# Three of six key chunks transposed by TensorE, one shared ring of four PSUM banks, and routing on GpSimd spread over later steps

## The chip, the cores and the metric

The kernel runs on one core of a Trainium2 chip. What counts is the device time of one launch, in microseconds (us). The core has a matrix engine (TensorE, PE in the profile), three engines for elementwise work (VectorE: DVE, ScalarE: ACT, GpSimd: POOL), a queue processor (SyncE: SP) and 16 DMA engines. Each engine runs its own list of instructions in the order in which the program wrote them, and waits at an instruction until the semaphores that it names have been reached.

## The reference

The kernel fuses an attention with a routed two-layer network. Four batches of 12288 queries (C = 128) look at 768 keys each, which are 4 by 4 means of `kv` times `w_sr`:

```python
kv_pool = kv.reshape(B, H // r, r, W // r, r, C).mean(axis=(2, 4))
k = v = kv_pool.reshape(B, -1, C) @ w_sr
s = (q @ k.transpose(0, 2, 1)) / np.sqrt(C)
a = np.exp(s - s.max(-1, keepdims=True))
a /= a.sum(-1, keepdims=True) + 1e-09
x = (a @ v).reshape(B * N, C)
do_compute = x @ w_skip > 0
out = x.copy()
# rows with do_compute: the best of 8 experts by x @ w_gate
out[rows of e] += gate_w * (np.maximum(x[rows of e] @ w1[e], 0) @ w2[e])
```

## The kernel before, in words

**Stages.** From about 36 us to 1107 us a loop runs over 384 tiles of 128 queries (96 per batch). Each tile's attention is computed, its rows are written to `out`, and after every 12 tiles a group is routed: for each active row the expert and the place in that expert's list are worked out, and the rows are scattered into a scratch array in HBM. From 1107 to 1205 us a first piece of the experts runs, and a device loop does the rest up to 1964 us. The change touches the first stage, and beyond it only the banks from which the first piece of the experts takes its PSUM tiles.

**One step.** Step t of the loop works on several tiles at once; the order in the program is the order on each engine:

- PE: `scores(t)`, six f32 matmuls of 128 x 384 (L578 to L580) into `s_ps`, which holds two tiles; `attend(t-6)`, 18 f16 matmuls (L641) whose weights are the transposed probabilities; `p_transpose(t-1)` (L616).
- DVE: `nm`, the row maximum of `scores(t)` (L586); then `ptq` lo (L624), the inverse of the row sums `rs` (L649, L651) and `p` lo (L599).
- ACT: `q_hi` (L566, every fourth step), `ptq` hi (L623), `p` hi (L595), the scaling of finished rows (L656, two tiles at a time), the exponential `p_sb` (L591).
- SP: a DMA transpose of `p16` into `pt` (L603) each step, and the transfers of q, kv, out and of padding rows.
- POOL: `q_lo` (L567), sums over kv blocks (L437, not in all steps), the routing (L692 to L708, L721, L756 to L760), row numbers (L771, L772), and 12 scatters for each group (L183, two emitted per step).

**Two ways to turn a tile.** The probabilities of a tile are a 128 x 768 f32 array and must be turned, so that keys lie on partitions: six chunks of 128. Each is kept as a sum of two f16 values, hi and lo. `KD` chunks are split first (`p` hi by ACT, `p` lo by DVE, side by side in `p16`) and turned by a DMA; the other `KP = KC - KD` are turned in f32 by PE into a PSUM bank and split from there (`ptq` hi by ACT, `ptq` lo by DVE). `PP` tiles share one bank and one pair of split instructions.

**PSUM.** `s_ps` has four banks. Before, `ps_a` has three banks that serve in turn, one for the attention results of each pair of tiles and one for the PE transposes of each pair; `ps_m` has one bank, "misc", for routing (31 groups) and for the preparation of the next batch's keys. A tile's next owner waits until its last readers are done: for attention results these are L649 and the two L656, for transposes L623 and L624.

**Routing.** `route(r, ...)` is a generator; each `yield` ends its work for the step. Its product `oh_all` (L721, POOL) is the operand of two matmuls at the end of a later step (L748, L749 on PE), whose results go through `pre` (L752, DVE) and POOL to `di`, the row numbers for the scatters.

Of the kernel before, what the change touches and what calls it, by code (L numbers as in the profile page):

```python
# [9 lines left out]
F32 = mybir.dt.float32  # L10
# [5 lines left out]
ALU = mybir.AluOpType  # L16
# [8 lines left out]
def kernel(  # L25
# [40 lines left out]
    LAG = 6  # L66
    W1, W2, W3 = 3, 6, 0
    PSL = 11
    KD = 4
    PP = 2  # L70
    L1, L2, PW, PX = 11, 8, 1, 1
    ROW = C + 4

# [291 lines left out]
    with ExitStack() as p1:  # L365
# [3 lines left out]
        qt = p1.enter_context(tc.tile_pool(name="qt", bufs=3))  # L369
        pp = p1.enter_context(tc.tile_pool(name="pp", bufs=3))  # L370
        ptp = p1.enter_context(tc.tile_pool(name="ptp", bufs=LAG))
        ptq = p1.enter_context(tc.tile_pool(name="ptq", bufs=4))
        hl = p1.enter_context(tc.tile_pool(name="hl", bufs=4))
        small = p1.enter_context(tc.tile_pool(name="small", bufs=6))
        rowp = p1.enter_context(tc.tile_pool(name="rowp", bufs=3))
        rt = p1.enter_context(tc.tile_pool(name="rt", bufs=3))
        ps_a = p1.enter_context(tc.tile_pool(name="ps_a", bufs=3, space=PSUM))
        ps_m = p1.enter_context(tc.tile_pool(name="ps_m", bufs=1, space=PSUM))
        started = []

        def acc_ps():
            return ps_a.tile([P, 512], F32, name="acc_ps")

        def misc_ps():
            return ps_m.tile([P, 512], F32, name="misc") if started else acc_ps()
        p_kv = p1.enter_context(ExitStack())
        kvp = p_kv.enter_context(tc.tile_pool(name="kvp", bufs=4))
        p_s = p1.enter_context(ExitStack())
# [162 lines left out]
            q_sb[g] = qp.tile([P, GW], F32, name="q_sb")  # L551
            nc.sync.dma_start(q_sb[g], q[r][:, o * GT:(o + 1) * GT, :].rearrange("c t p -> c (t p)"))

        early_a, early_g, late_a, early_v, jobs = [], [], [], [], []
        LASTR = NTILE // RT - 1
        SNAPR = LASTR - 4

        def run_late(q):
            while q:
                q.pop(0)()  # L560

        def q_split(g):
            q_g = q_sb.pop(g)
            hi = qt.tile([P, GW], F32R, name="q_hi")
            lo = qt.tile([P, GW], F32R, name="q_lo")
            early_a.append(lambda: nc.scalar.copy(hi, q_g))  # L566
            early_g.append(lambda: nc.gpsimd.tensor_tensor(out=lo, in0=q_g, in1=hi.bitcast(F32), op=ALU.subtract))  # L567
            qT[g] = (hi, lo)

        def scores(t):  # L570
# [98 lines left out]
        def route(r, a, b, last, eng):  # L669
# [27 lines left out]
            if few:  # L697
                eng.scalar_tensor_tensor(out=ev, in0=d, scalar=0.0, in1=em(em8), op0=ALU.is_equal, op1=ALU.mult)
                eng.tensor_scalar(out=act, in0=rows[:, :, C], scalar1=0.0, scalar2=None, op0=ALU.is_gt)
                eng.scalar_tensor_tensor(out=na, in0=rows[:, :, C], scalar=0.0, in1=idt[:, 0:n], op0=ALU.is_le,  # L700
                                         op1=ALU.mult)
                ohb = oh_few[a // GT % 2]
            else:
                eng.tensor_scalar(out=ev, in0=d, scalar1=0.0, scalar2=None, op0=ALU.is_equal)
                eng.tensor_tensor(out=ev, in0=ev, in1=em(em8), op=ALU.mult)
                eng.tensor_scalar(out=act, in0=rows[:, :, C], scalar1=0.0, scalar2=None, op0=ALU.is_gt)
                eng.tensor_scalar(out=na, in0=act, scalar1=-1.0, scalar2=1.0, op0=ALU.mult, op1=ALU.add)
                eng.tensor_tensor(out=na, in0=na, in1=idt[:, 0:n], op=ALU.mult)  # L708
                oha = oh_all[r % 3]
                ohb = oha.rearrange("p e t -> p t e")[:, 1:RTP, :]  # L710
            yield
# [7 lines left out]
            oh = big_t("oh")  # L719
            nc.vector.tensor_tensor(out=oh, in0=em(em8), in1=bc(mn), op=ALU.is_equal)  # L720
            eng.tensor_tensor(out=ohb[:, 0:n, :], in0=oh, in1=bc(act), op=ALU.mult)  # L721
            for _ in range(1 if few else 2 if r < LASTR - 1 else K2):
                yield
            yield (None if r >= LASTR - 1 else GT - 1)
            while accs.get("done", 0) != r * RT + a:
# [9 lines left out]
            if few:  # L735
                ohf = ohb.rearrange("p t e -> p (t e)")
                nc.tensor.matmul(ps[:, 0:w + E], upper_bf, ohf[:, 0:w + E], start=True, stop=False)
                for j in range(n):
                    nc.tensor.matmul(ps[:, (j + 1) * E:w + E], ones_bf,
                                     ohb[:, j:j + 1, :].broadcast_to([P, n - j, E]), start=False, stop=(j == n - 1))  # L740
                nc.vector.tensor_tensor(out=nxt, in0=run, in1=ps[:, w:w + E], op=ALU.add)
                nc.vector.tensor_tensor(out=acc, in0=ps[:, 0:w].rearrange("p (t e) -> p t e", e=E), in1=em(run),
                                        op=ALU.add)
                nc.vector.tensor_scalar(out=gs, in0=gs, scalar1=1e-9, scalar2=x_sc, op0=ALU.add, op1=ALU.mult)
            else:
                wa = E * RTP
                ohf = oha.rearrange("p e t -> p (e t)")
                nc.tensor.matmul(ps[:, 0:wa], ones_bf, ohf, start=True, stop=True)  # L748
                nc.tensor.matmul(ps[:, wa:2 * wa], upper_bf, ohf, start=True, stop=True)  # L749
                yield  # L750
                pre = rt.tile([P, E, RTP], F32, name="pre")
                nc.vector.tensor_tensor_scan(pre.rearrange("p e t -> p (e t)"), keep.rearrange("p e t -> p (e t)"),  # L752
                                             ps[:, 0:wa], 0.0, ALU.mult, ALU.add)
                inner = ps[:, wa:2 * wa].rearrange("p (e t) -> p t e", t=RTP)[:, 1:RTP, :]
                nc.vector.tensor_tensor(out=acc, in0=inner, in1=pre.rearrange("p e t -> p t e")[:, 0:RT, :], op=ALU.add)
                eng.tensor_tensor(out=nxt, in0=run, in1=pre[:, :, RT], op=ALU.add)  # L756
                eng.tensor_scalar(out=gs, in0=gs, scalar1=1e-9, scalar2=x_sc, op0=ALU.add, op1=ALU.mult)
                eng.tensor_tensor(out=acc, in0=acc, in1=em(run), op=ALU.add)
            accs["done"] = r * RT + b
            eng.tensor_tensor(out=acc, in0=acc, in1=ohb[:, 0:n, :], op=ALU.mult)  # L760
            yield
            nc.vector.reciprocal(rows[:, :, C], gs)
            yield
            if r == SNAPR:
# [117 lines left out]
        q_split(0)  # L882
        q_split(1)
        run_late(early_a)
        warm(W1)
        kv_transpose(0, KC - 1, KC)
        run_late(early_g)
# [2 lines left out]
        warm(W3)  # L890
        preps = [prep_v(0)]
        next(preps[0])
        started.append(True)
        pools = []
        if SNAPR < 0:
            snapshot(None)
# [12 lines left out]
        while t < NTILE + LAG - 1 or jobs:  # L909
            t += 1  # L910
            b, tb = divmod(t, TPB)
            live = t < NTILE
            for now, nxt in ((split_a, next_a), (split_v, next_v), (late_a, next_l)):
                now.extend(nxt)
                nxt.clear()
            if live:
                scores(t)
            if 0 <= t - LAG < NTILE:
                attend(t - LAG)
            if 0 <= t - 1 < NTILE:  # L920
                p_transpose(t - 1)
            if live:
                row_max(t)
            run_late(early_a)
            run_late(split_a)
            if 0 <= t - 1 < NTILE:
                p_hi(t - 1)
            run_late(late_a)
            if live:
                row_exp(t)  # L930
            run_late(early_g)
            run_late(split_v)
            run_late(early_v)
            if 0 <= t - 1 < NTILE:
                p_lo(t - 1)
            if live:
                if t % GT == 0 and t // GT + RG < NGRP:
                    load_q(t // GT + RG)
                if b + 1 < B:
                    for k, r in KV_T.get(tb, ()):  # L940
                        load_kv(b + 1, k, [r])
                if b + 1 < B and tb == PREP_T:
                    preps.append(prep_kv(b + 1))
                if t in PAD_T:
                    write_pads(*PADS.pop(0))
            first_step(NTILE - t)
            if t == NTILE:
                p_s.close()
                p_kv.close()
                alloc_h(p1.enter_context(tc.tile_pool(name="hp1", bufs=1)))  # L950
                ps_up = p1.enter_context(tc.tile_pool(name="ps_up", bufs=4, space=PSUM))
                alloc["h"] = lambda: ps_up.tile([P, ST], F32, name="up_ps")
            ph = t % GT
            if ph == 1 and t // GT + 2 < NGRP:
                q_split(t // GT + 2)
            ranked = run_jobs(ph)
            if preps and not ranked and (ph in (0, 3) or tb < LAG):
                if next(preps[0], "end") == "end":
                    preps.pop(0)
            if live and b + 1 < B:  # L960
                for k, r in KV_T.get(tb - 4, ()):
                    if r == R - 1:
                        pools.append(pool_kv(b + 1, k))
                for _ in range(2 if tb >= 74 else 1):
                    if pools and next(pools[0], "end") == "end":
                        pools.pop(0)
            for _ in range(2 * (t >= NTILE)):
                next(first)
# [77 lines left out]
```

## Time and profile before

| | us |
|---|---|
| median of three runs (1979.64, 1980.99, 1993.7) | 1980.99 |
| profiled execution, whole | 1965.99 |
| its span | 1964.2 |
| loop over the tiles, 36 to 1107 us: PE / DVE / ACT / POOL busy | 974 / 899 / 810 / 752 of 1071 |
| first piece of the experts, 1107 to 1205 us: PE busy | 67 of 98 |
| loop over the experts, 1205 to 1964 us: PE busy | 744 of 759 |

Busy time is the time in which an engine worked on instructions; what lies between them is idle, and the trace names for each idle stretch the event that ended it ("issue" where it sees none, "remote" where the event was not the end of a recorded instruction). The granted clock ("PEclk") is the share of full speed at which PE was let run. In a row of a timeline the first number is the start, the second the length; "x2" means two instructions drawn as one, and the bracket at the end holds the idle time before them.

### The profile page before, as it was taken

Reading aid. Unit: us, or ns where it says so; the run is one execution under the profiler, and the core shown is the slowest. Engines: PE = TensorE matmul, PEld = TensorE weight load, DVE = VectorE, ACT = ScalarE, POOL = GpSimd, SP = SyncE. Lnnn points to the kernel's source line nnn. Section 1 sums busy time; section 2 is a strip of 40 time slices with the busy share of each in tenths; the row PEclk is TensorE's granted clock in tenths of the full one; section 3 lists DMA queues with packets and bytes.
Section 4 is the critical chain, followed back from the end, with each engine's and each line's share of the span. In section 5 each row is a group of like instructions: output and inputs, shape, how many; then the busy total and the mean of one; then the engine's idle time right before and its main releaser. Section 6 shows DMA issues by size and latency. Waiting matters only on the chain. (4 is left out here: it accounts for less than half of the span.)

```text
span 1964.2 us, 42746 instructions
## 1 busy us (share of the span) xinstructions
PE 1795.4 (91%) x13955; PEld 1284.2 (65%) x13955; DVE 1567.7 (80%) x3226; ACT 1325.5 (67%) x2484; POOL 1092.2 (56%) x1372
## 2 busy tenths in 40 slices
PE   4999978999898999898988768999999999999997
PEld 3988878988788888787887623444444444444443
DVE  7999967989877999686787736887878788878786
ACT  3878866878777878676776624666666666666664
POOL 2378864888857888656556552333333333333333
PEclk9999989999999999899999878999999999999999
DMA  7999978999888999799998613333333433333343
GB/s 173 205 199 213 202 164 165 211 180 187 158 160 167 201 205 208 159 195 183 180 181 187 133 50 104 92 97 92 97 90 99 111 98 93 95 94 95 90 99 90
DMA packets 621971, 284.88 MB, mean 145 GB/s; under 512 B 503168, under 2 KB 571904, under 8 KB 621824
## 3 DMA queue, kind: packets, MB, share of 16 engines
q1 hardware_dynamic: 600320, 244.56, 61.0%
q0 software_dynamic: 21504, 38.43, 6.8%
q8 instruction: 83, 1.36, 0.3%
q14 instruction: 64, 0.52, 0.1%
HBM read 90.60 MB, written 78.64 MB: 86 GB/s over the span
## 5 line engine op out<-in xcount | busy, mean ns | idle before, releaser
L183 POOL DMA_INDIRECT out_dram<-o,xin x288 | 295.9, 1028 | 494.9 <-DVE o L292 428.7
L591 ACT ACTIVATE p_sb<-s_ps,nm 128x768 f32<-128x768 f32 x384 | 346.9, 903 | 184.4 <-DVE nm L586 155.8
L183 POOL DMA_INDIRECT scr<-rows,di x384 | 394.9, 1028 | 135.4 <-issue 107.0
L586 DVE TENSOR_REDUCE nm<-s_ps 128x1 f32<-128x768 f32 x384 | 363.7, 947 | 125.0 <-PE s_ps L580 68.0
L269 DVE SCALAR_TENSOR_TENSOR h_lo<-h_ps,h_hi 128x512 f16<-128x512 f32 x544 | 344.1, 685 | 146.2 <-ACT h_hi L268 109.2
L641 PE MATMUL acc_ps<-v_hi,pt 128*128 128x138 f16 x3072 | 331.9, 228 | 48.1 <-DVE rs L649 24.1
L641 PEld LDWEIGHTS <-pt 128*128 128x128 f16 x4608 | 286.9, 100 | 121.1 <-issue 120.6
L268 ACT ACTIVATE h_hi<-h_ps 128x512 f16<-128x512 f32 x544 | 318.4, 597 | 51.2 <-PE h_ps L267 32.2
L599 DVE SCALAR_TENSOR_TENSOR p<-p_sb,p 128x512 f16<-128x512 f32 x384 | 318.2, 829 | 1.9 <-ACT p L595 1.4
L641 PE MATMUL acc_ps<-v_lo,pt 128*128 128x138 f16 x1536 | 302.6, 227 | 0.5 <-issue 0.5
L578 PE MATMUL s_ps<-k_hi,q_hi 128*128 128x384 f32 x768 | 299.2, 390 | 3.5 <-issue 3.4
L579 PE MATMUL s_ps<-k_lo,q_hi 128*128 128x384 f32 x768 | 265.4, 346 | 4.2 <-issue 4.0
L580 PE MATMUL s_ps<-k_hi,q_lo 128*128 128x384 f32 x768 | 264.3, 344 | 2.2 <-issue 2.2
L595 ACT ACTIVATE p<-p_sb 128x512 f16<-128x512 f32 x384 | 242.4, 631 | 7.4 <-DMA pt<-p 4.2
L265 PE MATMUL h_ps<-xT,w_hi 128*128 128x512 f16 x544 | 207.1, 381 | 6.0 <-issue 6.0
L266 PE MATMUL h_ps<-xT,w_hi 128*128 128x512 f16 x544 | 207.0, 380 | 0.0
L267 PE MATMUL h_ps<-xT,w_lo 128*128 128x512 f16 x544 | 206.9, 380 | 0.0
L281 PE MATMUL y_ps<-h_hi,w_hi 128*128 128x512 f16 x544 | 206.2, 379 | 0.0
L281 PE MATMUL y_ps<-h_hi,w_lo 128*128 128x512 f16 x544 | 206.2, 379 | 0.0
L281 PEld LDWEIGHTS <-w_hi 128*128 128x128 f16 x1152 | 113.4, 98 | 134.5 <-issue 4.0
L281 PE MATMUL y_ps<-h_lo,w_hi 128*128 128x512 f16 x544 | 195.1, 379 | 0.0
L284 ACT ACTIVATE yT<-y_ps,y_sc 128x512 f32<-128x512 f32 x68 | 46.7, 687 | 219.5 <-PE y_ps L281 219.5
(215 smaller groups left out, 3215.5 us busy)
## 6 DMA issues: line engine op xcount, KB each, us to landing
kvt<-in_kv_dram SPq DMA_DIRECT2D x96, 256.0 KB
q_sb<-in_q_dram SPq DMA_DIRECT2D x96, 256.0 KB
out_dram<-rows SPq DMA_DIRECT2D x96, 256.0 KB
xin<-scr SPq DMA_DIRECT2D x75, 264.0 KB, 2.9
w_raw<-in_moe_w_dram SPq DMA_DIRECT2D x38, 512.0 KB
scr<-pad SPq DMA_DIRECT2D x32, 264.0 KB
pt<-p SPq DMA_TRANSPOSE x384
scr<-rows,di POOLq DMA_INDIRECT x384
```

The costliest lines, as they stand in the source:

```text
L183: ins = nc.gpsimd.indirect_dma_start(out=dst, out_offset=bass.IndirectOffsetOnAxis(ap=ids, axis=0), in_=src, in_offset=None, bounds_check= ...
L268: nc.scalar.activation(out=h["hi"][:, c, :], in_=ps, func=AF.Relu)
L269: nc.vector.scalar_tensor_tensor(out=h["lo"][:, c, :], in0=ps, scalar=0.0, in1=h["hi"][:, c, :], op0=ALU.max, op1=ALU.subtract)
L281: nc.tensor.matmul(ps, w[:, c, :], h[x][:, c, :], start=(i == 0), stop=(i == len(terms) - 1))
L578: nc.tensor.matmul(s[:, h, :HK], q_hi, k_hi[:, sl], start=True, stop=False)
L579: nc.tensor.matmul(s[:, h, :HK], q_hi, k_lo[:, sl], start=False, stop=False)
L580: nc.tensor.matmul(s[:, h, :HK], q_lo, k_hi[:, sl], start=False, stop=True)
L586: nc.vector.tensor_reduce(out=NM[t], in_=S_PS[t][:, :, :HK], axis=AX.XY, op=ALU.max, negate=True)
L591: nc.scalar.activation(out=P_SB[t], in_=S_PS.pop(t)[:, :, :HK], func=AF.Exp, bias=NM.pop(t))
L595: nc.scalar.activation(out=P16[t][:, 0, :], in_=p_flat(t)[:, 0:KD * P], func=AF.Copy, scale=2.0 ** PEXP)
L599: nc.vector.scalar_tensor_tensor(out=p16[:, 1, :], in0=p_flat(t)[:, 0:KD * P], scalar=2.0 ** PEXP, in1=p16[:, 0, :], op0=ALU.mult, op1=ALU ...
L641: nc.tensor.matmul(ps[:, j % 2, :], w, v[a][:, k, :], start=(i == 0), stop=(i == len(AVL) - 1))
```

## The change

- `KD` goes from 4 to 3 and `PP` from 2 to 1: PE turns three chunks of every tile, not two; `ptq` is split for every tile (384 columns), not for every second (512); `p` hi, `p` lo and the DMA transposes work on 384 columns, not 512. `ptq` has 6 buffers in place of 4.
- `ps_a` and `ps_m` become one pool of four banks. Attention results, PE transposes and misc tiles take the next bank in turn.
- On ACT the scaling of finished rows comes ahead of `ptq` hi and `p` hi.
- `q_lo` is put into a list `next_g` that moves into `early_g` at the start of the following step.
- In `route`, `na` is one instruction; the part behind L752 (`nxt`, `gs`, `acc`) starts a step later, the reciprocal and the scatters two steps later; one more `yield` stands between `oh_all` and the matmuls.

```diff
-    KD = 4
-    PP = 2
+    KD = 3
+    PP = 1
...
-        ptq = p1.enter_context(tc.tile_pool(name="ptq", bufs=4))
+        ptq = p1.enter_context(tc.tile_pool(name="ptq", bufs=LAG))
...
-        ps_a = p1.enter_context(tc.tile_pool(name="ps_a", bufs=3, space=PSUM))
-        ps_m = p1.enter_context(tc.tile_pool(name="ps_m", bufs=1, space=PSUM))
-        started = []
-
+        ps_a = p1.enter_context(tc.tile_pool(name="ps_a", bufs=4, space=PSUM))
         def acc_ps():
             return ps_a.tile([P, 512], F32, name="acc_ps")
 
         def misc_ps():
-            return ps_m.tile([P, 512], F32, name="misc") if started else acc_ps()
+            return acc_ps()
...
             early_a.append(lambda: nc.scalar.copy(hi, q_g))
-            early_g.append(lambda: nc.gpsimd.tensor_tensor(out=lo, in0=q_g, in1=hi.bitcast(F32), op=ALU.subtract))
+            next_g.append(lambda: nc.gpsimd.tensor_tensor(out=lo, in0=q_g, in1=hi.bitcast(F32), op=ALU.subtract))
...
                 eng.tensor_scalar(out=act, in0=rows[:, :, C], scalar1=0.0, scalar2=None, op0=ALU.is_gt)
-                eng.tensor_scalar(out=na, in0=act, scalar1=-1.0, scalar2=1.0, op0=ALU.mult, op1=ALU.add)
-                eng.tensor_tensor(out=na, in0=na, in1=idt[:, 0:n], op=ALU.mult)
+                eng.tensor_scalar(out=na, in0=rows[:, :, C], scalar1=0.0, scalar2=float(BIG), op0=ALU.is_le, op1=ALU.mult)
...
-            for _ in range(1 if few else 2 if r < LASTR - 1 else K2):
+            for _ in range(1 if few else 3 if r < LASTR - 1 else K2):
                 yield
...
+                if r < LASTR - 1:
+                    yield
                 eng.tensor_tensor(out=nxt, in0=run, in1=pre[:, :, RT], op=ALU.add)
...
             yield
+            if not few and r < LASTR - 1:
+                yield
             nc.vector.reciprocal(rows[:, :, C], gs)
...
-            for now, nxt in ((split_a, next_a), (split_v, next_v), (late_a, next_l)):
+            for now, nxt in ((split_a, next_a), (split_v, next_v), (late_a, next_l), (early_g, next_g)):
...
             run_late(early_a)
+            run_late(late_a)
             run_late(split_a)
             if 0 <= t - 1 < NTILE:
                 p_hi(t - 1)
-            run_late(late_a)
             if live:
                 row_exp(t)
             run_late(early_g)
```

Lines behind the pools move up by three in the changed kernel (L721 becomes L717, L748 becomes L744).

On POOL, this stands before, for one group in the second batch, from the scatters of the group ahead of it (L183, `di`) over the routing's first part (L692 to L708) to `oh_all`:

```order
L183 DMA scr<-rows,di 409600x132 x2
L692 TENSOR_TENSOR d<-lg,mx 128x96
L704 TENSOR_SCALAR ev<-d 128x96
L705 TENSOR_TENSOR ev<-ev,em_80 128x96
L706 TENSOR_SCALAR act<-rows 128x12
L707 TENSOR_SCALAR na<-act 128x12
L708 TENSOR_TENSOR na<-na,idt 128x12
L183 DMA scr<-rows,di 409600x132 x6
L567 TENSOR_TENSOR q_lo<-q_sb,q_hi 128x512
L183 DMA scr<-rows,di 409600x132 x2
L721 TENSOR_TENSOR oh_all_94<-oh,act 128x12x8
L183 DMA scr<-rows,di 409600x132 x2
```

And this stands there in the changed kernel:

```order
L689 TENSOR_TENSOR d<-lg,mx 128x96
L701 TENSOR_SCALAR ev<-d 128x96
L702 TENSOR_TENSOR ev<-ev,em_80 128x96
L703 TENSOR_SCALAR act<-rows 128x12
L704 TENSOR_SCALAR na<-rows 128x12
L771 COPY rows<-x_sc 128x12
L772 IOTA rows 128x12
L183 DMA scr<-rows,di 409600x132 x4
L564 TENSOR_TENSOR q_lo<-q_sb,q_hi 128x512
L183 DMA scr<-rows,di 409600x132 x2
L717 TENSOR_TENSOR oh_all_94<-oh,act 128x12x8
L183 DMA scr<-rows,di 409600x132 x6
```

All of the scatters of the group ahead now stand behind the routing's first part; six of the twelve stand ahead of `oh_all`, ten before; and six come behind it, two before. `q_lo` has kept its place between the scatters.

On ACT, this is the order of some four steps before (L656 scaled rows, L591 exponential, L623 `ptq` hi, L595 `p` hi, L566 `q_hi`):

```order
L656 ACTIVATE rows<-acc_ps,rs 128x138 x2
L591 ACTIVATE p_sb<-s_ps,nm 128x768
L623 ACTIVATE ptq<-acc_ps 128x512
L595 ACTIVATE p_7639<-p_sb 128x512
L591 ACTIVATE p_sb<-s_ps,nm 128x768
L566 CAST q_hi<-q_sb 128x512
L595 ACTIVATE p_7686<-p_sb 128x512
L656 ACTIVATE rows<-acc_ps,rs 128x138 x2
```

And the like in the changed kernel:

```order
L653 ACTIVATE rows<-acc_ps,rs 128x138 x2
L620 ACTIVATE ptq<-acc_ps 128x384
L592 ACTIVATE p_6951<-p_sb 128x384
L588 ACTIVATE p_sb<-s_ps,nm 128x768
L620 ACTIVATE ptq<-acc_ps 128x384
L592 ACTIVATE p_7009<-p_sb 128x384
L588 ACTIVATE p_sb<-s_ps,nm 128x768
L563 CAST q_hi<-q_sb 128x512
L653 ACTIVATE rows<-acc_ps,rs 128x138 x2
```

The rows of a pair stand at the head of their step now, ahead of both splits, and `ptq` hi stands in every step. On PE the two transposes of a step (L616) become three (L613), at the same place between `attend` and the next `scores`.

More of the change, by code (lines that the diff above doesn't have):

```diff
@@ L552, in load_q @@
             nc.sync.dma_start(q_sb[g], q[r][:, o * GT:(o + 1) * GT, :].rearrange("c t p -> c (t p)"))
-        early_a, early_g, late_a, early_v, jobs = [], [], [], [], []
+        early_a, early_g, next_g, late_a, early_v, jobs = [], [], [], [], [], []
         LASTR = NTILE // RT - 1
@@ L884 @@
         run_late(early_a)
+        early_g.extend(next_g)
+        next_g.clear()
         warm(W1)
@@ L892 @@
         next(preps[0])
-        started.append(True)
         pools = []
```

## The prediction

> **What bounds the kernel now.** The page gives the whole first: PE is busy nine tenths of the span, and nearly all that the DMA queue q1 moves belongs to the attention stage.
>
> ```profile
> span 1964.2 us, 42746 instructions
> ...
> PE 1795.4 (91%) x13955; PEld 1284.2 (65%) x13955; DVE 1567.7 (80%) x3226; ACT 1325.5 (67%) x2484; POOL 1092.2 (56%) x1372
> ...
> q1 hardware_dynamic: 600320, 244.56, 61.0%
> ```
>
> The change lies in the loop, so I cut that into stretches, and counted the steps of each by its row maxima. The first table has the busy time of all engines, granted clock and DMA share; in the second the number in brackets is the steps.
>
> ```profile
> 36.00:216.00 180.00, 170.78 (x1805) 156.87 (x1806) 165.75 (x298) 148.88 (x270) 116.75 (x153) 1.00 1.02 198
> 216.00:362.00 146.00, 128.56 (x1276) 116.10 (x1276) 114.44 (x221) 103.07 (x190) 99.05 (x135) 0.93 0.89 175
> 362.00:486.00 124.00, 117.84 (x1259) 108.39 (x1257) 114.90 (x208) 100.59 (x185) 106.96 (x141) 0.99 1.01 191
> 486.00:628.00 142.00, 127.90 (x1289) 116.52 (x1287) 113.97 (x223) 103.23 (x191) 99.83 (x135) 0.94 0.81 159
> ...
> 752.00:1107.00 355.00, 313.40 (x3161) 284.15 (x3159) 276.05 (x557) 254.60 (x468) 224.62 (x300) 0.95 0.89 181
> ```
> ```profile
> 36.00:216.00 180.00, 68.19 (x73) 1.00 1.02 198
> 216.00:362.00 146.00, 45.45 (x48) 0.93 0.89 175
> 362.00:486.00 124.00, 45.42 (x48) 0.99 1.01 191
> 486.00:628.00 142.00, 45.66 (x49) 0.94 0.81 159
> ...
> 752.00:1107.00 355.00, 113.54 (x120) 0.95 0.89 181
> ```
>
> There are two kinds of stretch. The smooth ones (36 to 216, 362 to 486; the one from 628 to 752 is like the latter) take 180/73 = 2.47 and 124/48 = 2.58 us a step, with PE busy for 95% and DVE for 92%. The broken ones (48, 49 and 120 steps, 217 in all) take 146 + 142 + 355 = 643 us, 2.96 a step, with less busy time on every engine and a lower clock. What a step takes when PE never waits is read from PE's timeline:
>
> ```profile
> 644.15 0.42 PE L578 MATMUL s_ps<-k_hi,q_hi 128*128 128x384 f32 x1
> ...
> 645.30 0.29 PE L641 MATMUL acc_ps<-v_hi,pt 128*128 128x138 f16 x2
> ...
> 646.39 0.38 PE L616 MATMUL acc_ps<-ident,p_sb 128*128 128x128 f32 x2
> 646.53 0.43 PE L578 MATMUL s_ps<-k_hi,q_hi 128*128 128x384 f32 x1
> ```
>
> From one `scores` to the next it is 646.53 - 644.15 = 2.38 us: scores 1.15, attend 1.09, transposes 0.14 before the next row starts. So the broken stretches lose 643 - 217 x 2.38 = 127 us. Of these PE is idle for 17.4 + 14.1 + 41.6 = 73; the clock that is 7, 6 and 5% down is worth 10 + 9 + 18 = 37; the rest is other work of PE. The recoverable sum is thus about 110.
>
> The idle part has two sources. One is a wait of the routing, once per group:
>
> ```profile
> PE misc L748 <- POOL oh_all L721: 23.2, 15, 4.0
> ```
> ```profile
> 528.44 0.62 POOL L721 TENSOR_TENSOR oh_all<-oh,act 128x96 bf16<-128x96 f32 x1
> ...
> 529.11 0.25 PE L748 MATMUL misc<-oh_all,ones_bf 128*128 128x104 bf16 x1 [4.04 <-POOL oh_all L721]
> ```
>
> The other isn't tied to a named wait. The first table here has three neighbouring stretches of 6 us, the rows behind it what lies in the middle one.
>
> ```profile
> 919.00:925.00 6.00, 6.00 (x64) 5.51 (x63) 5.12 (x11) 5.38 (x10) 4.60 (x8) 1.00 1.06 220
> 925.00:931.00 6.00, 2.39 (x24) 1.92 (x21) 0.98 (x2) 1.12 (x2) 4.92 (x5) 1.00 1.04 217
> 931.00:937.00 6.00, 5.27 (x47) 5.14 (x48) 3.56 (x7) 3.65 (x7) 3.77 (x5) 0.72 0.62 131
> ```
> ```profile
> 926.56 0.98 POOL L183 DMA_INDIRECT scr<-rows,di  x1 [0.30 <-issue]
> ...
> 927.49 0.34 PE L580 MATMUL s_ps<-k_hi,q_lo 128*128 128x384 f32 x1
> ...
> 927.85 0.97 POOL L183 DMA_INDIRECT scr<-rows,di  x1 [0.31 <-issue]
> ...
> 930.02 0.96 DVE L586 TENSOR_REDUCE nm<-s_ps 128x1 f32<-128x768 f32 x1 [5.46 <-remote]
> ...
> 931.73 0.39 PE L641 MATMUL acc_ps<-v_hi,pt 128*128 128x138 f16 x2 [3.90 <-DVE rs L649]
> ```
>
> PE, DVE and ACT all stop while the DMA engines are full (1.04) and POOL issues scatters without a break, 1.29 us apart (927.85 - 926.56). Afterwards the clock is 0.72. I read it as a glut of transfers that holds up signals; that is a reading, since smooth stretches have the same DMA share (1.01, 1.02) without such stops.
>
> **The change part by part.** The prices come from these groups (mean ns is the last number before the second bar).
>
> ```profile
> L586 DVE TENSOR_REDUCE nm<-s_ps 128x1 f32<-128x768 f32 x384 | 363.7, 947 | 125.0 <-PE s_ps L580 68.0 <-PE acc_ps L641 22.7 <-remote 22.3
> ...
> L591 ACT ACTIVATE p_sb<-s_ps,nm 128x768 f32<-128x768 f32 x384 | 346.9, 903 | 184.4 <-DVE nm L586 155.8 <-issue 22.2 <-DVE p L599 2.7
> ...
> L595 ACT ACTIVATE p<-p_sb 128x512 f16<-128x512 f32 x384 | 242.4, 631 | 7.4 <-DMA pt<-p 4.2
> ...
> L599 DVE SCALAR_TENSOR_TENSOR p<-p_sb,p 128x512 f16<-128x512 f32 x384 | 318.2, 829 | 1.9 <-ACT p L595 1.4 <-ACT p_sb L591 0.5
> ...
> L616 PE MATMUL acc_ps<-ident,p_sb 128*128 128x128 f32 x768 | 151.5, 280 | 7.5 <-ACT p_sb L591 4.5 <-issue 2.4
> ...
> L623 ACT ACTIVATE ptq<-acc_ps 128x512 f16<-128x512 f32 x192 | 113.7, 592 | 52.9 <-PE acc_ps L641 25.3 <-remote 19.4 <-PE s_ps L580 5.1
> ...
> L624 DVE SCALAR_TENSOR_TENSOR ptq<-acc_ps,ptq 128x512 f16<-128x512 f32 x192 | 130.8, 681 | 0.7 <-ACT ptq L623 0.7
> ...
> L649 DVE TENSOR_SCALAR rs<-acc_ps,v_sc 128x2 f32<-128x2 f32 x192 | 40.5, 211 | 31.5 <-PE acc_ps L641 14.7 <-PE acc_ps L616 7.0 <-PE up_ps L267 3.5
> ...
> L656 ACT ACTIVATE rows<-acc_ps,rs 128x138 f32<-128x138 f32 x384 | 121.3, 369 | 16.2 <-DVE rs L651 8.0 <-PE up_ps L267 3.1 <-DVE rs L649 1.9
> ```
>
> *PE.* One transpose more per tile. The pair takes 0.38 us from its start to its end and one alone 0.28 (L616's mean, which overlaps the neighbour), so a further one adds 0.38 - 0.28 = 0.10; 151.5 us over 384 pairs, 0.395 each, gives 0.115. I take 0.11, or 384 x 0.11 = 42 us, and a bare step of 2.49. In the broken stretches PE is back to back between stops (6.00 of 6), so 217 x 0.11 = 24 lie on the path. In 362 to 486 there are 124 - 117.84 = 6.2 us of idle PE for 48 x 0.11 = 5.3: covered, but by so little that I charge half for its two like stretches (5), and 6 for the first 73 steps, whose pace of 2.47 is below 2.49. Together **+35**.
>
> The Trainium skill, "TensorE: Matmul & The Clock Gate", Part 4 on transposes, puts one at about 275 ns in a kernel's context; by that the term would be 384 x 0.275 = 106, not 42. The duration in L616's row agrees, the spacing in the timeline doesn't.
>
> *ACT.* `p` hi loses a quarter of its columns. From L623 and L656 a column costs (592 - 369)/(512 - 138) = 0.6 ns, at most 631/512 = 1.2: 77 to 158 ns less. `ptq` hi becomes 592 - 128 x 0.6 = 515 for each tile instead of 296. Net +0.06 to +0.14 us a step; ACT has 100.59 of 124 busy, which hides it.
>
> *DVE.* Likewise `ptq` lo: from L624 and L649 a column costs (681 - 211)/510 = 0.92 ns, so 563 a tile for 340, +0.22; `p` lo loses 0.12 to 0.21. Net +0.01 to +0.10 a step. DVE has 9 us free over 48 steps, 0.19 each. I take nothing; without that cover it would be up to 10 x 3.84 = 38.
>
> *DMA.* Each transposed array of 128 x 1024 f16 (262 KB) shrinks by a quarter: 384 x 65.5 KB = 25 MB of q1's 244.56, a tenth of the bytes; SP's queue keeps its order.
>
> *Routing.* Four scatters fewer stand ahead of `oh_all`, which comes 4 x 1.29 = 5.2 us earlier against the same matmul; the longest wait was 4.0. So all 23.2 us can go, with the clock that follows them (110/73 of it: 35). Next late are the six scatters that now follow, on which no engine waits. Since some waits lie in smooth stretches, I take **-25**, bounds 0 and -35. `nxt` a step later frees POOL of a wait, nothing else. `q_lo` stays where it was, in the step of its `q_hi`: no price.
>
> *Stops under the DMA glut.* 110 - 35 = 75 us are left. The lighter transposes act on their cause if my reading is right, the scatters that stay dense keep it if not. Bounds 0 and -75; I take 0.7 of it, nearer to the full DMA row (1.04) than to the smooth rows, **-52**.
>
> *One ring of banks.* In plain steps the order is one attention bank and two transpose banks per pair. The transposes of an even step then need the bank whose rows ACT scales in that same step. `nm` ends 1.15 + 0.95 us into the step before, the exponential 0.90 later, at 0.62 of this step; two rows of 0.37 end at 1.36; the transposes start at 2.24 (646.39 - 644.15). That is 0.9 us of slack, so no price. Whenever a misc tile is drawn (31 times for routing, about 28 for keys, counted in the code), the next attention bank is the last one, and attend at 1.15 waits for rows at 1.36: 59 x 0.21 = **+12**. A wait of that kind in the trace costs more:
>
> ```profile
> PE acc_ps L641 <- DVE rs L649: 24.1, 28, 3.9
> ```
>
> 24.1/28 = 0.86 each; as upper bound 59 x 0.86 = 51. Behind a waiting attend stand that step's transposes and the next scores, and DVE and ACT behind those. That ACT scales rows earlier makes this wait shorter and delays `ptq` hi by 0.74 us, which is used four steps later. The first piece of the experts draws on the same ring; I price that at nothing.
>
> Sum: +35 - 25 - 52 + 12 = **-30 us**, so 1966 becomes 1936 for an execution like the profiled one. That one lies 15 below the median of 1981; against the median I expect **1951**.
>
> **Rivals.** *A, the forecast* (chance 0.50): most of the stops go. With all gone and no ring wait it is 35 - 35 - 75 = -75, 1906.
>
> *B, the stops stay* (0.25): they come from dense scatters, not from the load of transposes. For: the smooth rows with a DMA share of 1.01 and 1.02; against: the stop's own 1.04. The added transposes fall partly inside the stops, so I charge 20 of 35: -25 + 20 + 12 = +7, **1988**. The Trainium skill, "SBUF — State Buffer", in its part on ports and who waits for whom, says that a DMA never contends with a compute engine. By that rule the relief of the DMA would give nothing; the stop at 925 shows PE still with DMA full, so the trace leaves it open.
>
> *C, the ring paces PE* (0.20), on the slower side. The 0.9 us of slack holds only if DVE takes `nm` at once; with 92% of DVE busy, an `nm` behind `ptq` lo and `p` lo (0.56 + 0.65) is over a microsecond late, the exponential and the rows behind it in ACT too, and PE waits before its transposes. From that delay on, one row per pair shows: 192 x 0.37 = 71 in place of 12. With 0.4 of the stops gone: 35 - 25 - 30 + 71 = +51, **2032**.
>
> *D, transposes at full length* (0.05). If the third one costs L616's whole 0.28, PE's term is 108, the path's about 35 x 108/42 = 90 instead of 35: -30 + 55 = +25, **2006**. Against it speak the starts 646.39 and 646.53. The Trainium skill's page on TensorE, named above, would have it so.
>
> **How the numbers follow.** A change of 1%, 20 us, is what a measurement of this kernel can tell from none. A (1906 to 1990 by its fraction of the stops) is faster in nine tenths of its cases: 0.45; B in a tenth, same in 0.17 of its 0.25; C and D are slower but for 0.04. Faster 0.47, same 0.27, slower 0.26. The range reaches from A's best with a little lost, 1900, to between D and C, 2015.
>
> **What would show it.** Right: three transposes 0.11 apart and a bare step of 2.49; hardly a wait of PE for `oh_all`; broken stretches near 2.6 a step at a clock near 1. Wrong: stops of 5 us at the same places (B); waits of L638 or L613 for ACT's `rows` over 50 us (C); a bare step over 2.6 (D).

## The result

| | before | changed |
|---|---|---|
| median, us | 1982.91 (4 runs) | 2051.57 (4 runs, 2047.62 to 2057.55) |
| ratio, 95% interval | | 1.0354 [1.0313, 1.0396] |
| profiled execution, whole / span | 1965.99 / 1964.2 | 2057.55 / 2055.7 |
| PE busy in the span | 1795.4 | 1869.0 |

The kernel became 3.5% slower, where 1.6% faster was forecast. Four more executions on another occasion (f1 below) gave a median of 2025.53 us and a ratio of 1.0292 [1.0246, 1.0338], so the loss is real and its size differs by half a per cent from one occasion to the other. Below are the parts of the page of the changed kernel that answer to those shown.

```profile
span 2055.7 us, 43981 instructions
...
PE 1869.0 (91%) x14339; PEld 1344.1 (65%) x14339; DVE 1557.6 (76%) x3418; ACT 1326.6 (65%) x2676; POOL 1057.3 (51%) x1341
...
q1 hardware_dynamic: 502016, 219.40, 50.3%
```

q1 moves 25.2 MB less (244.56 before), as worked out, and its share of the engines fell from 61.0 to 50.3%. The DMA got lighter and the kernel slower. The next rows are the windows of two stretches of the changed kernel, all engines first and then the row maxima, whose count is the steps. The first holds about the same tiles as 362 to 486 before, the second the last 143 steps.

```profile
382.00:527.00 145.00, 131.25 (x1318) 120.16 (x1316) 111.70 (x233) 102.91 (x211) 101.58 (x138) 0.94 0.71 141
754.00:1201.00 447.00, 397.54 (x3919) 356.99 (x3918) 334.35 (x732) 307.10 (x630) 272.15 (x361) 0.94 0.72 153
```
```profile
382.00:527.00 145.00, 45.74 (x49) 0.94 0.71 141
754.00:1201.00 447.00, 136.25 (x143) 0.94 0.72 153
```

The stretch that was smooth (2.58 us a step at clock 0.99) now takes 145/49 = 2.96 at 0.94: it is as broken as the rest. An undisturbed step is what was worked out; on PE's timeline it reads

```profile
441.45 0.49 PE L613 MATMUL acc_ps<-ident,p_sb 128*128 128x128 f32 x3
441.70 0.43 PE L575 MATMUL s_ps<-k_hi,q_hi 128*128 128x384 f32 x1
...
443.94 0.49 PE L613 MATMUL acc_ps<-ident,p_sb 128*128 128x128 f32 x3
444.19 0.43 PE L575 MATMUL s_ps<-k_hi,q_hi 128*128 128x384 f32 x1
```

444.19 - 441.70 = 2.49, and three transposes take 0.49 where two took 0.38 or 0.39. So the loss lies in the disturbed steps. The waits by name show where, and where not:

```profile
POOL nxt L754 <- DVE pre L748: 133.1, 28, 12.4
...
PE acc_ps L638 <- issue: 70.2, 110, 2.1
...
PE acc_ps L613 <- ACT rows L653: 7.1, 9, 2.3
```

PE's wait for `oh_all`, 23.2 us before, is gone from the list. The wait for ACT's rows, on which rival C rested, is 7 us. What grew is the second row: PE stands in the middle of `attend`, where it waits for nothing that the profile shows. Before, this was

```profile
PE acc_ps L641 <- issue: 11.9, 18, 1.2
```

Such a place in the changed kernel, in windows of 6 us and in the timeline of all engines:

```profile
418.00:424.00 6.00, 6.00 (x71) 5.68 (x69) 4.42 (x9) 4.72 (x10) 5.03 (x6) 1.00 0.65 132
424.00:430.00 6.00, 2.56 (x15) 1.39 (x14) 2.85 (x4) 2.20 (x5) 4.97 (x5) 0.98 0.45 115
430.00:436.00 6.00, 5.49 (x35) 5.11 (x35) 4.54 (x10) 3.60 (x8) 2.14 (x3) 0.50 0.37 71
```
```profile
421.52 1.01 POOL L183 DMA_INDIRECT scr<-rows,di  x1
...
422.84 0.97 POOL L183 DMA_INDIRECT scr<-rows,di  x1 [0.30 <-issue]
...
424.11 1.21 POOL L183 DMA_INDIRECT scr<-rows,di  x1 [0.30 <-issue]
...
424.66 0.34 PE L577 MATMUL s_ps<-k_hi,q_lo 128*128 128x384 f32 x1 [0.34 <-issue]
...
425.40 0.34 PE L575 MATMUL s_ps<-k_hi,q_hi 128*128 128x384 f32 x1 [0.41 <-issue]
...
425.63 0.97 POOL L183 DMA_INDIRECT scr<-rows,di  x1 [0.30 <-issue]
...
426.15 0.34 PE L576 MATMUL s_ps<-k_lo,q_hi 128*128 128x384 f32 x1 [0.41 <-issue]
...
426.90 0.97 POOL L183 DMA_INDIRECT scr<-rows,di  x1 [0.30 <-issue]
...
427.58 0.22 PE L638 MATMUL acc_ps<-v_hi,pt 128*128 128x138 f16 x1 [0.84 <-issue]
...
428.17 0.98 POOL L183 DMA_INDIRECT scr<-rows,di  x1 [0.30 <-issue]
...
428.34 0.22 PE L638 MATMUL acc_ps<-v_lo,pt 128*128 128x138 f16 x1 [0.36 <-issue]
```

Six scatters start 1.3 to 1.5 us apart. From the third on, three matmuls of a chain start 0.74 us apart (424.66, 425.40, 426.15) where 0.17 is the pace, and the ones behind them come a few at a time, with 0.36 to 0.84 us of idle time between. The window counts 15 matmuls where the one before it counts 71. DVE and ACT have little to do behind it, and in the 6 us after it PE gets half of its clock (0.50). The DMA engines are at 0.45 meanwhile, less than half of what the stop at 925 us had before (1.04). That fells the reading on which the prediction's largest term rested. Over the whole loop, first before and then in the changed kernel, the clock went from 0.96 to 0.94 and the DMA share from 0.93 to 0.72:

```profile
36.00:1107.00 1071.00, 974.04 (x10016) 887.82 (x10016) 898.63 (x1711) 809.68 (x1483) 751.65 (x999) 0.96 0.93 184
```
```profile
35.00:1201.00 1166.00, 1051.44 (x10407) 949.74 (x10408) 891.43 (x1901) 818.79 (x1674) 722.19 (x973) 0.94 0.72 148
```

The loop is 95 us longer; PE is busy for 77 of them and idle for 18. Of the 77, 50 are the third transpose (below). The other 27 are the matmuls of `scores` and `attend`, as many as before, taking longer at the lower clock (L575 398 ns in the mean, where it was L578 with 390 before).

### The profile page after: what moved, and what is told of

It reads as the page before. It is cut to its first block, busy times and chain, and to the rows that moved or that the text cites. A ratio compares the mean times of both kernels' runs of the same rounds, so it can differ in the third digit from the quotient of the medians.

```text
span 2055.7 us, 43981 instructions
## 1 busy us (share of the span) xinstructions
PE 1869.0 (91%) x14339; PEld 1344.1 (65%) x14339; DVE 1557.6 (76%) x3418; ACT 1326.6 (65%) x2676; POOL 1057.3 (51%) x1341
## 3 DMA queue, kind: packets, MB, share of 16 engines
q1 hardware_dynamic: 502016, 219.40, 50.3%
## 5 line engine op out<-in xcount | busy, mean ns | idle before, releaser
L183 POOL DMA_INDIRECT out_dram<-o,xin x288 | 295.2, 1025 | 503.6 <-DVE o L292 437.5
L183 POOL DMA_INDIRECT scr<-rows,di x384 | 392.7, 1023 | 170.9 <-issue 161.8
L575 PE MATMUL s_ps<-k_hi,q_hi 128*128 128x384 f32 x768 | 306.0, 398 | 2.5 <-issue 2.2
L638 PE MATMUL acc_ps<-v_hi,pt 128*128 128x138 f16 x2304 | 266.0, 229 | 29.7 <-issue 21.6
L638 PEld LDWEIGHTS <-pt 128*128 128x128 f16 x3456 | 214.9, 100 | 113.2 <-issue 111.4
L638 PE MATMUL acc_ps<-v_hi,ptq 128*128 128x138 f16 x2304 | 259.7, 227 | 25.7 <-issue 25.7
L638 PEld LDWEIGHTS <-ptq 128*128 128x128 f16 x3456 | 229.9, 99 | 46.7 <-issue 46.5
L596 DVE SCALAR_TENSOR_TENSOR p<-p_sb,p 128x384 f16<-128x384 f32 x384 | 243.2, 633 | 0.5 <-ACT p_sb L588 0.3
L620 ACT ACTIVATE ptq<-acc_ps 128x384 f16<-128x384 f32 x384 | 189.4, 493 | 83.9 <-PE acc_ps L613 37.8
L638 PE MATMUL acc_ps<-v_lo,ptq 128*128 128x138 f16 x1152 | 231.9, 227 | 12.1 <-issue 12.0
L638 PE MATMUL acc_ps<-v_lo,pt 128*128 128x138 f16 x1152 | 231.8, 227 | 11.1 <-issue 10.9
L613 PE MATMUL acc_ps<-ident,p_sb 128*128 128x128 f32 x1152 | 201.8, 284 | 21.4 <-issue 8.7
L621 DVE SCALAR_TENSOR_TENSOR ptq<-acc_ps,ptq 128x384 f16<-128x384 f32 x384 | 210.4, 548 | 4.6 <-ACT ptq L620 2.6
```

What stands on the lines that cost most here:

```text
L183: ins = nc.gpsimd.indirect_dma_start(out=dst, out_offset=bass.IndirectOffsetOnAxis(ap=ids, axis=0), in_=src, in_offset=None, bounds_check= ...
L575: nc.tensor.matmul(s[:, h, :HK], q_hi, k_hi[:, sl], start=True, stop=False)
L596: nc.vector.scalar_tensor_tensor(out=p16[:, 1, :], in0=p_flat(t)[:, 0:KD * P], scalar=2.0 ** PEXP, in1=p16[:, 0, :], op0=ALU.mult, op1=ALU ...
L621: next_v.append(lambda: nc.vector.scalar_tensor_tensor(out=hl_t[:, 1, :], in0=ps, scalar=2.0 ** PEXP, in1=hl_t[:, 0, :], op0=ALU.mult, op1 ...
L638: nc.tensor.matmul(ps[:, j % 2, :], w, v[a][:, k, :], start=(i == 0), stop=(i == len(AVL) - 1))
```

## The experiments

**Which part of the change costs it?** Theory R: the later routing puts the scatters into a dense row in which PE slows. Theory T: the third transpose and the split of every tile. Theory S: the shared ring. (Theory L, further below, is that the later routing delays something that PE needs.) Two kernels take one part out of the change, two make one part alone. The tiles back (e1), from the changed kernel; the tiles alone (e2) are the reverse edit, from the kernel before:

```diff
-    KD = 3
-    PP = 1
+    KD = 4
+    PP = 2
...
-        ptq = p1.enter_context(tc.tile_pool(name="ptq", bufs=LAG))
+        ptq = p1.enter_context(tc.tile_pool(name="ptq", bufs=4))
```

The routing back (e3), from the changed kernel; the routing alone (e4) is the reverse, from the kernel before:

```diff
-            for _ in range(1 if few else 3 if r < LASTR - 1 else K2):
+            for _ in range(1 if few else 2 if r < LASTR - 1 else K2):
...
-                if r < LASTR - 1:
-                    yield
                 eng.tensor_tensor(out=nxt, in0=run, in1=pre[:, :, RT], op=ALU.add)
...
-            if not few and r < LASTR - 1:
-                yield
             nc.vector.reciprocal(rows[:, :, C], gs)
```

> The changed kernel with four DMA chunks and pairs of tiles again (KD 4, PP 2, four ptq buffers); the shared ring, ACT's order and the later routing stay. Theory R (the later routing puts the scatters into a dense row in which PE's issue slows): the loss stays, 2030 to 2060 us. Theory T (the third transpose and the split of every tile cost it): back to 1975 to 2000. Theory S (the shared ring): stays, and PE's waits for ACT's rows with it.

> The kernel before with three DMA chunks and single tiles (KD 3, PP 1, six ptq buffers), separate banks, old routing steps. Theory R: 1960 to 2000 us, since the scatters stand where they stood. Theory T: 2030 to 2060. Theory S: as R.

> The changed kernel with the old routing steps (two yields ahead of the matmuls, none ahead of nxt, one ahead of the reciprocal); tiles, ring and ACT's order stay. Theory R: most of the loss goes, 1960 to 2000 us. Theory T and theory S: 2030 to 2060.

> The kernel before with only the three additional yields of the routing. Theory R: 2020 to 2060 us, the scatters in a dense row in stretches that were smooth. Theory T and theory S: 1970 to 1990.

A later run made the last corner, ring and order without the other two:

> The kernel before with the shared ring, the earlier rows on ACT and the shorter na alone: four DMA chunks, pairs of tiles, old routing steps, two scatters per step. It is the corner that lacks between the kernels with two and three parts of the change. If the parts add up (tiles 0, routing +10 on this ring), 1950 to 1965 us. If tiles and routing cost only together, 1940 to 1955.

Measured, as ratios to the kernel before on the same chip (S: shared ring, ACT's order, the shorter `na` and the list of `q_lo`; T: tiles; R: later routing):

| kernel | parts | median, us | ratio, 95% interval |
|---|---|---|---|
| e4_routing_alone | R | 1977.14 | 1.0052 [1.0018, 1.0087] |
| e2_tiles_alone | T | 2019.16 | 1.0257 [1.0211, 1.0304] |
| g3_ring_and_order_alone | S | 1952.38 | 0.9846 [0.9787, 0.9906] |
| e1_tiles_back | S, R | 1965.57 | 0.9973 [0.9948, 0.9997] |
| e3_routing_back | S, T | 1958.5 | 0.9956 [0.9934, 0.9979] |
| f1_after_again | S, T, R | 2025.53 | 1.0292 [1.0246, 1.0338] |

No theory holds alone: e1 lies outside what each of the three had expected, and R alone (e4) costs half a per cent where theory R had over 2%. Both e1 and e3 are back at the kernel before: on the shared ring each of T and R may be there, not both. There T costs 1.1% and R 1.3% (from 0.9846), together 4.5% in f1. And S, which the prediction charged with 12 us, gains 1.5%. The interval of g3 is 0.6% to either side, so the parts of one per cent are rough, and its 1952.38 us lies in both of the ranges expected for it; the 4.5% is clear.

e2 missed theory R's 1960 to 2000 and theory T's 2030 to 2060, for a reason of its own. A pair now needs one attention bank and two transpose banks, out of three. They are not handed out strictly in turn: in e2's program the first transposes of a pair take the bank of the attention tile before, whose rows ACT scales in that same step, for 188 of the 192 pairs. These are the waits for it:

```profile
PE acc_ps L616 <- ACT rows L656: 44.5, 86, 2.5
```

This is rival C's mechanism, with a wait at 86 of 192 pairs. In the change, with a fourth bank, there are 9.

**Is it the row of scatters?** One scatter per step instead of two (in the first 26 groups), and four, in kernels that are otherwise those above. First the line of f2 (from the changed kernel) and f3 (from e3), then that of f5 (from e3):

```diff
-                if j % 2 == 0 and j > 0 and r < LASTR - 1:
+                if j > 0 and (j % 2 == 0 or r < SNAPR - 1) and r < LASTR - 1:
                     yield
```
```diff
-                if j % 2 == 0 and j > 0 and r < LASTR - 1:
+                if j % 4 == 0 and j > 0 and r < LASTR - 1:
```

> The changed kernel, unaltered, beside the runs that follow. All theories: 3 to 4% over the kernel before on this chip. If it comes out within 1% of it, the first measurement's interaction of tiles and routing needs another reason.

> The changed kernel with one scatter emitted per step instead of two in the first 26 groups; the number of scatters and all else stay. Theory R (four or more scatters back to back slow PE's issue): the pauses of PE under scatters fall from 130 us to under 60, and the time to 1950 to 2000 us. Theory L (the later routing delays something that PE needs, such as bank or rows, and scatters only happen to lie there): no better than the changed kernel, 2030 or more.

> The changed kernel with the old routing steps and one scatter per step in the first 26 groups. Theory R: the 55 us of pauses that this kernel had at two per step fall to under 30; 1915 to 1950 us, faster than the kernel before. Theory L: as at two per step, 1950 to 1965.

> The changed kernel with the old routing steps and four scatters emitted per step instead of two. Theory R: longer rows of scatters without a break, more pauses, 1980 to 2030 us. Theory L: as at two per step, 1950 to 1965.

| kernel | median, us | ratio, 95% interval | PE `attend` <- issue, us (times) |
|---|---|---|---|
| f3_routing_back_one_per_step | 1911.55 | 0.9692 [0.9658, 0.9725] | 15.7 (24) |
| e3_routing_back, two per step | 1958.5 | 0.9956 [0.9934, 0.9979] | 28.2 (46) |
| f5_routing_back_four_per_step | 2050.86 | 1.0389 [1.0351, 1.0426] | 58.0 (109) |
| f1_after_again, two per step | 2025.53 | 1.0292 [1.0246, 1.0338] | 38.5 (76) |
| f2_after_one_per_step | 2045.52 | 1.0377 [1.0343, 1.0412] | 13.0 (22) |

The dose answers: from f3 to e3 to f5, kernels that are alike but for the scatters per step, the time rises by 2.6 and 4.3% of the kernel before, clear of the intervals. The stops in `attend` about double each time; they come from one trace each, and two traces of the changed kernel itself have 70.2 and 38.5 us, so the times carry the argument. Theory L had f3 at 1950 to 1965 and falls; theory R had the direction right and the size too small, both ways (1915 to 1950 for f3, 1980 to 2030 for f5). The stops by themselves don't set the time, though. e1, with the later routing and four DMA chunks, has as many as f1 and stands at 0.9973:

```profile
PE acc_ps L638 <- issue: 38.8, 72, 2.0
```

f1 is 2.9% over the kernel before, where 3 to 4 was expected. f2 missed theory R's 1950 to 2000: its stops went, its time didn't come down. The waits of f2 say why:

```profile
ACT rows L653 <- DMA scr<-rows,di: 114.4, 25, 5.8
```

Twelve scatters over twelve steps that begin two steps later end where the rows of the group three further on are first written, into the same one of three buffers. A fourth buffer should mend it (g1); and the kernels with four DMA chunks got one scatter per step as well (f4 from the kernel before, g5 from g3, the line as in f2). The edit of g1, from f2:

```diff
-        rowp = p1.enter_context(tc.tile_pool(name="rowp", bufs=3))
+        rowp = p1.enter_context(tc.tile_pool(name="rowp", bufs=4))
```

> The changed kernel with one scatter per step and four buffers for the rows of a group instead of three. Its sister with three buffers had 114 us of waits of ACT's rows for the scatters of the group three before. Theory R (dense rows of scatters slow PE; that sister only lost it to the buffers): 1900 to 1935 us, no waits of rows for scatters. Theory L (the later routing itself delays): 2000 us or more.

> The kernel before with one scatter per step in the first 26 groups, nothing else. Theory R: its 76 us of pauses and part of the waits behind them shrink to a third, 1915 to 1945 us; then the third transpose is worth little by itself. If it stays at 1960 to 1975, the gain of the one-per-step kernel needs the three chunks or the shared ring.

> The kernel of the run before with one scatter per step. Theory R: 1895 to 1925 us. Beside the same with three DMA chunks (1911.6) it shows what the third transpose is worth once the pauses are gone: at 1900 or less it is a loss of 10 or more, above 1920 a gain.

| one scatter per step | parts | median, us | ratio, 95% interval | beside two per step |
|---|---|---|---|---|
| f4_before_one_per_step | none | 1926.39 | 0.9717 [0.9656, 0.9778] | 1 |
| g5_ring_and_order_one_per_step | S | 1917.35 | 0.9670 [0.9613, 0.9727] | 0.9846 |
| f3_routing_back_one_per_step | S, T | 1911.55 | 0.9692 [0.9658, 0.9725] | 0.9956 |
| g1_after_one_per_step_4_rows | S, T, R | 1930.51 | 0.9737 [0.9681, 0.9794] | 1.0292 |

Once the rows of scatters are broken up, the parts hardly matter: all four lie within 0.7%, and all beat both kernels, the kernel before with its one line changed among them. What T is worth there is too small to be told (0.9670 and 0.9692, intervals overlapping). From f1 to g1, with one scatter per step and one buffer more, 5.5 hundredths come back, and theory L, which had g1 at 2000 or more, falls here too. The buffer by itself was not run with two scatters per step; f1 has no wait of ACT's rows for scatters, so it has nothing of that kind to take away there.

**Spacing or place?** Spreading also moves the scatters to other steps. The last kernel leaves them in their steps and their order and puts useless work on GpSimd behind each:

```diff
+        filler = consts.tile([P, 512], F32, name="filler")
...
                 scatter_rows(scr, di[:, j:j + 1], rows[:, j, 0:ROW], E * CAP - 1, "scr")
+                if r < SNAPR - 1:
+                    nc.gpsimd.memset(filler, 0.0)
```

> The changed kernel with a filling of 128 x 512 f32 on GpSimd (about 0.5 us, no use) behind each scatter of the first 26 groups; two scatters per step, the same steps, the same order. Scatters in a row are then about 1.8 us apart instead of 1.27. Theory R (what slows PE is how close scatters follow one another): the pauses in the middle of PE's chains fall to under half although GpSimd has more to do; the time falls below 2010 us unless GpSimd becomes the bound. Theory P (what matters is how long GpSimd is occupied beside PE, or where in the group the scatters lie): pauses as before or more, 2050 us or more.

Measured: 1981.12 us, 1.0055 [1.0036, 1.0074], where the changed kernel stands at 1.0292 and 1.0354. Work that computes nothing made the kernel over 2% faster, each by its ratio to the kernel before on its chip. On its timeline scatters in a row are 1.67 us apart, and a window of 6 us over the end of that row has PE without a gap (the 6 us before it hold the end of a wait for `oh_all`, and a clock of 0.72):

```profile
412.62 0.97 POOL L183 DMA_INDIRECT scr<-rows,di  x1 [0.17 <-issue]
413.58 0.55 POOL L779 MEMSET filler<- 128x512 f32 x1
414.29 0.97 POOL L183 DMA_INDIRECT scr<-rows,di  x1 [0.17 <-issue]
```
```profile
413.00:419.00 6.00, 6.00 (x74) 5.69 (x72) 5.63 (x8) 4.48 (x10) 5.67 (x8) 1.00 0.68 156
```
```profile
PE acc_ps L745 <- POOL oh_all L718: 43.8, 16, 4.7
...
PE acc_ps L639 <- issue: 11.4, 19, 1.7
```

The stops in `attend` are at 11.4 us (38.5 and 70.2 without the filling), and 43.8 us of a wait came in their place that the change had removed: `oh_all` stands behind the filling now. So it is the spacing of the scatters that counts, and theory P falls: in this kernel's loop GpSimd was busy for 82% of the time, more than in any other of these kernels.

## Why the prediction was wrong

It read the broken stretches rightly as what was worth most, and gave the stops in them the wrong cause. Of its two main gains (-25 and -52) nothing was left, and a term that it put at nothing was a loss. By its own steps:

- **The third transpose, +35.** About right. The bare step is 2.49 as forecast. Its group costs 201.8 us where L616 cost 151.5, 50 and not 42, part of it at a lower clock:

```profile
L613 PE MATMUL acc_ps<-ident,p_sb 128*128 128x128 f32 x1152 | 201.8, 284 | 21.4 <-issue 8.7
```

  On the shared ring the whole of T measures +1.1% (22 us) at two scatters per step.
- **`oh_all`, -25.** Right: the wait is gone. Nothing of it was kept, because of the next two steps.
- **"Next late are the six scatters that now follow, on which no engine waits."** This is the step that failed. No engine waits for them by a semaphore, and yet they hold up PE when they follow one another closely (f3, f5, h1). The term was nought. Where R is added to S and T, it costs 3.4% (0.9956 to 1.0292), some 67 us.
- **The stops, "a glut of transfers", -52.** Wrong. The change took a tenth of q1's bytes away and the DMA share of the loop fell from 0.93 to 0.72; the stops in `attend` went from 11.9 to 70.2 us. The prediction had seen the row that spoke against it (smooth stretches at a share of 1.01 and 1.02) and still set 0.7 of the stops as cured. What set the smooth stretches apart stood in the same trace, on POOL's timeline. Let a row of scatters go on as long as the next one starts within 1.55 us. Then the loop before has 11 rows of six, all in the broken stretches (2, 2 and 7), and no row longer than two in the three smooth ones, where more of GpSimd's key sums (L437) run: 32, 25 and 24, against 18, 18 and 11. The changed kernel has 18 rows of six or more, 13 of them of eight or more. The gain itself was also set too high: f4, which has no wait for `oh_all` and 6 us of stops in `attend` (11.9 before), is 40 to 60 us faster than the kernel before (1924.17 beside 1965.99 in the profiled executions, 1926.39 beside 1987.28 in the medians), about half of the 110 held for recoverable.
- **The ring, +12, and rows earlier on ACT, nought.** Sign wrong: S as a whole measures -1.5% [-2.1, -0.9]; which part of it gains was not taken apart. The order of banks was misread. In the changed program the bank whose rows ACT scales in a step goes to the transposes of that same step for 34 of the 192 pairs only, and for 145 to those of the step after. For most pairs the slack was thus a whole step more than the 0.9 us. Rival C came true with three banks, in e2, and hardly with four.
- **Rival B** had the right fact, that dense scatters make the stops, but the wrong price. It held the scatters' density for unchanged. The order on POOL that stands above has six scatters behind `oh_all` where two stood, with two directly ahead of it in both kernels; it was read only for what comes before `oh_all`. The Trainium skill, "SBUF — State Buffer", section "Who interferes with whom", says that a DMA never contends with a compute engine; the lower DMA share with more stops agrees with that. The same section, which is about ports of the SBUF, says that PE and ACT never wait on anyone; h1 shows that PE's pace hangs on how closely GpSimd issues scatters, so if the rule holds, the way from one to the other is not such a port.
- **Rival D** fell: 2.49 a step. The Trainium skill's figure ("TensorE: Matmul & The Clock Gate", Part 4, about 275 ns) agrees with the mean of one, 284; in a row a third one adds 0.11 us, and that is what the step pays.

Why T and R cost more together than apart (1.1 and 1.3%, against 4.5) is argued, not shown: before, PE had 124 - 117.84 = 6.2 us of idle time in a smooth stretch of 48 steps, which could take up stops; T uses 5.3 of it, and what R adds then falls on the path in full. The kernels with one scatter per step fit this. In f4's loop, without T, PE is idle for 1031 - 952 = 79 us; in f3's, with T, for 1017 - 985 = 32 (its row is at the end):

```profile
35.00:1066.00 1031.00, 952.11 (x10016) 871.26 (x10016) 921.67 (x1710) 808.09 (x1483) 781.73 (x1000) 0.99 0.96 191
```

So does e1, where as many stops as in f1 go with a loss of 1.3% (e1 beside g3) in place of 3.4% (f1 beside e3), and so do the four corners, which agree within 0.7% once the stops are gone.

What stays open is how a scatter slows PE. No run here shows it. In the stretch from 424 to 430 us the scatters moved next to no bytes (160 packets of the software queue and 0.00 MB), so it isn't their data. In a like stop from 865 to 871 us, with 19 matmuls in the window, they moved 0.35 MB; there the instruction queues (q8 and q14) moved no packet, which speaks against the loading of instructions as the way. The row of the first:

```profile
q0 software_dynamic: 160, 0.00, 2.0%
```

## What to carry to other kernels

Before scatters (or any descriptors that GpSimd makes) are moved, look at what will stand between them, not only at who waits for them: in rows 1.3 us apart they cost several per cent of this kernel, and 1.7 us apart most of that was gone. A wait with no releaser in the middle of a chain of matmuls, in several kernels at the same neighbour, is a cause to be found by dose (one, two, four per step), not by its share of the DMA. And two parts of a change that are each nearly harmless can be costly together, perhaps because they share one reserve: take them out one by one, and make the corners.

## What the runs showed that was not expected

- While scatters start 1.3 to 1.5 us apart, PE starts 15 matmuls in 6 us instead of 71, some of them 0.74 us apart instead of 0.17, without any wait by name, at a DMA share of 0.45.
- After such a stop the granted clock is 0.50 over 6 us. Over the whole loop it is 0.94 in the changed kernel and 0.99 in f3, as the row of f3's loop shows:

```profile
36.00:1053.00 1017.00, 984.92 (x10395) 906.27 (x10395) 913.09 (x1902) 808.65 (x1674) 745.12 (x966) 0.99 0.84 169
```

- The filling's own row is that of the groups by line:

```profile
L779 POOL MEMSET filler<- 128x512 f32 x312 | 170.5, 546 | 0.4
```

  A filling of 0.55 us behind each scatter, 170 us of work in all (312 of 546 ns), took the changed kernel from 1.0292 or 1.0354 to 1.0055.
- One line of the kernel before, one scatter per step in place of two, gives 2.8% (f4, 0.9717 [0.9656, 0.9778]).
